# Gated mix of two attentions: the score maxima of two heads taken by one reduction over two adjacent PSUM banks

## The chip, the core and the metric

The kernel runs on one core of a Trainium2 chip. The metric is the device time of one launch in microseconds; lower is better. The core's engines work side by side, each through its own queue in order: TensorE (PE, with its weight loads listed apart as PEld), VectorE (DVE), ScalarE (ACT), GpSimd (POOL), and SyncE (SP), which issues most transfers. Matmuls write to PSUM, here used as eight banks of 128 partitions x 512 fp32 values.

## The reference

Two attentions are computed on the same input x (2048 tokens, width 512, 32 heads of 16), mixed by a gate per token:

```python
def _A_ref(x, wq, wk, wv, wo, beta):        # causal inside 4 segments of 512 tokens, plus a memory
    ...
    for s in range(N):
        logits = einsum("bhqd,bhkd->bhqk", qs, ks) * scale + mask
        p = softmax(logits); a_dot = einsum("bhqk,bhkd->bhqd", p, vs)
        num = einsum("bhld,bhde->bhle", phi(qs), M); den = einsum("bhld,bhd->bhl", phi(qs), z) + 1e-6
        outs.append(g * num / den + (1 - g) * a_dot)
        M = M + einsum("bhld,bhle->bhde", phi(ks), vs); z = z + phi(ks).sum()
    ...
def _B_ref(x, wqkv, wo):                    # full attention over 2048 tokens
    p = softmax(einsum("bhqd,bhkd->bhqk", q, k) * Dh ** -0.5)
    ...
g = sigmoid((x * gate_w).sum(-1, keepdims=True))
return g * _A_ref(...) + (1 - g) * _B_ref(...)
```

The softmax needs the maximum of each query's scores. The kernel computes the scores twice: once with the queries on the partitions, only for their maxima, and once transposed, with the maxima already subtracted inside the product, for the exponentials.

## The kernel before, in words

**Stages.** Up to about 366 us the projections, the memory part of attention A and the first maxima are computed. Then a long loop over k = 0..31 follows; step k of it (called a *unit* here) handles one set of four heads and 512 queries of attention B (number 32+k in the code) and one of attention A (number k). Units 0 to 30 have 25 *phases* each (`NPH`, p = 0..24). Unit 31 has no maxima left to compute and runs in another form, and a tail writes the last outputs.

**A phase** is one call of `step` and one of `pv_cols`. `step` emits two kinds of products. *T products* (`qk_mm`, L509; `a_unit`, L549 for attention A) are transposed scores of one head, 128 keys x 512 queries; ACT takes the exponential of each bank (L513, L552) and writes it to SBUF. There are three in a phase and they rotate over three banks, tb0, tb1 and mb. *S products* (`s_half`, L528; `s_a_half`, L425 for attention A) are scores of the *next* unit, 128 queries x 512 keys of one head, for the maxima; DVE reduces each bank to one maximum per query (L532; L445 and L447 for attention A). They rotate over four banks, sbk0 to sbk3 (`SK`, by `rot("s", SK)`). For attention A the causal mask is added by four small matmuls (`s_a_end`, L439 and L441) before the reduction. After `step`, `pv_cols` emits the *PV products* (`pv`, L626): exponentials times values, four heads at a time in four column groups, summed over the whole unit in the bank pvb.

**Row groups.** S and T products contract over only 64 partitions. `r = slice(64 * j, 64 * j + 64)` for an S product of half j, and `r = slice(64 * (h % 2), ...)` for a T product of head h, say which half of TensorE's rows it uses. An S item comes twice in the list of items, once for each half j, which are two heads. `step` asks for the half that is not the row group of the T product that follows (`s_item(f, 1 - n % 2)`).

**What sets the order.** It is written out by hand: the Python emits instructions in the order in which each engine runs them. `CP` says how many S products each phase holds: three in every phase, four in the last. `SAP` says which phases hold one of attention A's six items (phases 16, 7, 20, 13, 24, 0). From unit 9 on, phase `OMP` = 8 is followed by one output projection (`out_mm`, twelve full-width matmuls, L691) into a bank taken from the S rotation. Phase 13 ends with `m_chain` (L471, one small reduction on DVE), which marks one point of every unit in the trace. Phase 17 ends with `m_rows` (L488, small matmuls), and phases 1 and 22 with `fin_copy` (L635: ACT copies pvb out), which the next PV products wait for.

Of the kernel before, what the change touches and what calls it, by code (L numbers as in the profile page):

```python
# [7 lines left out]
FT = mybir.dt.float32  # L8
# [4 lines left out]
OP = mybir.AluOpType  # L13
AX = mybir.AxisListType
# [7 lines left out]
C = 512  # L22
# [10 lines left out]
def gated_mix_kernel(ctx, tc, x, wq, wk, wv, wo, beta, wqkv, wob, gate_w, out):  # L33
    nc = tc.nc
# [5 lines left out]
    PS = ctx.enter_context(tc.tile_pool(name="ps", bufs=1, space=PSUM))  # L40
# [41 lines left out]
    ones = P.tile([128, 1], FT, name="ones")  # L82
    MST = [[X.tile([128, 8, 32], FT, name=f"mst{i}{s}") for s in range(2)] for i in range(2)]

    TB = [PS.tile([128, C], FT, name=f"tb{i}") for i in range(2)]
    PVB = PS.tile([128, C], FT, name="pvb")
    MB = PS.tile([128, C], FT, name="mb")
    SK = [PS.tile([128, C], FT, name=f"sbk{i}") for i in range(4)]
    APVB = [PVB, MB]
    lru = []  # L90

# [4 lines left out]

    mode = {"misc": TB + [MB, PVB] + SK[::2]}

# [14 lines left out]
    def rot(key, lst):  # L113
        i = cnt.get(key, 0)
        cnt[key] = i + 1
        return lst[i % len(lst)]
# [301 lines left out]
    SAB = {}  # L418

    def s_a_half(u, i, p, j):  # L420
        n = 128 * (i + 1)
        b = SAB.setdefault((u, i, p), {})[j] = rot("s", SK)
        r = slice(64 * j, 64 * j + 64)
        for c0, q in [(0, p)] if p is not None else [(0, 0), (256, 1)]:
            nc.tensor.matmul(b[:, c0:c0 + n], q_of(u)[r, q, i * 128:(i + 1) * 128], k_of(u, q)[r, :n],  # L425
                             start=c0 == 0, stop=False, skip_group_check=True)

    def s_a_end(u, i, p):
        mx = pair_max(chain_of(u))
        n = 128 * (i + 1)  # L430
        bs = SAB.pop((u, i, p))
        np = 1 if p is not None else 2
        for n2 in (1, 0):
            for j in (1, 0):
                r = slice(64 * j, 64 * j + 64)
                d = bs[j].rearrange("q (p k) -> q p k", p=np)[:, :, n - 128 + 64 * n2:n]
                mv = cmask[r, n2, None, 64 * n2:].to_broadcast([64, np, 128 - 64 * n2])
                if n2:
                    nc.tensor.matmul(d, crows[r, 1], mv, start=False, stop=False, skip_group_check=True)  # L439
                else:  # L440
                    nc.tensor.matmul(d[:66], crows[r, 0, :66], mv, start=False, stop=True, skip_group_check=True)  # L441
        m = mx[:, 0].rearrange("q (j p) i -> q j p i", j=2)
        for j in bs:
            if np == 1:
                nc.vector.tensor_reduce(m[:, j, p, i:i + 1], bs[j][:, :n], axis=AX.X, op=OP.max)  # L445
            else:
                nc.vector.tensor_reduce(m[:, j, :, i], bs[j].rearrange("q (p k) -> q p k", p=2)[:, :, :n], axis=AX.X,  # L447
                                        op=OP.max)

    def s_a(u, i, p):  # L450
        for j in (1, 0):
# [3 lines left out]
    MXB = {}  # L455
# [63 lines left out]
    def s_half(t, j=None):  # L519
        u, i, p, kc = t  # L520
        js = HALF.setdefault(t, [1, 0])
        if j in js:
            js.remove(j)
        else:
            j = js.pop(0)
        b = rot("s", SK)
        r = slice(64 * j, 64 * j + 64)
        nc.tensor.matmul(b, q_of(u)[r, p, i * 128:(i + 1) * 128], k_of(u, p)[r, kc * C:(kc + 1) * C],  # L528
                         start=True, stop=True)
        if u not in MXB:  # L530
            MXB[u] = W.tile([128, 2, 2, 4, 4], FT, name="mxb")
        nc.vector.tensor_reduce(MXB[u][:, j, p, i, kc:kc + 1], b, axis=AX.X, op=OP.max)  # L532

    def s_item(f, j=None):
        if callable(f):
            f()
        elif f[0] == "A":
            s_a_half(*f[1:], j)
        else:
            s_half(f, j)  # L540
# [15 lines left out]

    NPH = 25

    def step(k, ns, items, banks):
        for n in ns:  # L560
            ends = None
            if items:
                f = items.pop(0)
                s_item(f, 1 - n % 2)
                if not callable(f) and f[0] == "A":
                    SEEN[f] = SEEN.get(f, 0) + 1
                    ends = f if SEEN[f] == 2 else None
            if n < 64:
                it, h = divmod(n, 4)
                b = bank(banks)  # L570
                qk_mm(32 + k, it, h, b)
                exp_b(32 + k, it, h, b)
            else:
                a_unit(k, n - 64, banks)
            if ends:
                s_a_end(*ends[1:])
        while items:
            f = items.pop(0)
            s_item(f)

    SEEN = {}

# [104 lines left out]
    def out_mm(c, t, a, b=None):  # L687

        b = misc() if b is None else b
        for n, (oi, wi, g) in enumerate([(oi, wi, g) for oi, wi in TERMS for g in range(4)]):  # L690
            nc.tensor.matmul(b, (AT["oh"], AT["ol"])[oi][:, g, a], (AT["wh"], AT["wl"])[wi][:, g, a],  # L691
                             start=n == 0, stop=n == 11)
        if a == 0:
            AT["yo"] = AT["L"].tile([128, DM], FT, name="yo")
            (nc.vector.tensor_copy if c == 2 and t == 3 else nc.scalar.copy)(AT["yo"], b)
        else:
            tt = 4 * c + t
            if tt == 11:
                nc.vector.tensor_tensor(AT["yo"], b, AT["yo"], op=OP.add)
            else:  # L700
                y2 = AT["L"].tile([128, DM], FT, name="y2")
                nc.scalar.activation(y2, b, AF.Copy)
                nc.gpsimd.tensor_tensor(AT["yo"], y2, AT["yo"], op=OP.add)
            nc.sync.dma_start(outr[tt * 128:(tt + 1) * 128, :], AT["yo"])
# [149 lines left out]
    for blk in range(16):  # L854
        g, c = divmod(blk, 4)
        pg, pc = divmod(blk - 1, 4)
        if blk == 4:
            mode["misc"] = TB + [MB, PVB]
        if 4 <= blk < 14:
# [5 lines left out]
        n = blk + 1 + (c == 2)  # L865
# [36 lines left out]
        for n in range(4):  # L902
# [9 lines left out]
            if nf == 35:  # L912
                mode["misc"] = [MB, PVB, TB[1]]
            if n < 3 and nf < want:
# [45 lines left out]

    T3 = TB + [MB]
    TAIL = [SK[n] for n in (2, 3, 0, 1)]
# [69 lines left out]

    ex = [extras(k) for k in range(32)]
    plan = {}
    CP = [3, 3, 3, 3, 3, 3, 3, 3, 3, 3, 3, 3, 3, 3, 3, 3, 3, 3, 3, 3, 3, 3, 3, 3, 4]
    PLAST = 14
    OM1, OM2 = 4, 10
    TMB = 18
# [14 lines left out]
    for k in range(31):  # L1053
# [15 lines left out]
        for n, t in enumerate(ST_A):  # L1069
            if True:  # L1070
                p = SAP[n]
# [35 lines left out]
    for k in range(32):  # L1107
        ua, ub = k, 32 + k
        if k == 31:
            for it in range(NT + 5):  # L1110
                step(k, range(4 * it, min(4 * it + 4, 74)), [], (T3 if it < NT - 4 else TB) + SK * (it < TMB) + TAIL[1:] * (it >= TMB))
                if it in (OM1, OM2):
                    out_mm(2, 3, int(it == OM2))
                n = it - 2
                if it == 0:
                    pv_cols(30, END - 256, END)
                    fin_copy(30)
                elif n >= 0:
                    lo, hi = (min(C * m, NT * C + (0, C, C + 512, C + 768)[max(m - NT, 0)]) for m in (n, n + 1))
                    pv_cols(k, lo, hi)  # L1120
                for a in TM.get(it, ()):
                    tail_mm(0, range(3), a)
                if n == NT - 1:
                    tail_hop(63)
                if it == 3:
                    m_chain(32)
                if it == 5:
                    m_rows(32)
                hooks(k, it)
            tail_hop(31)  # L1130
            continue
        done = 0
        for p in range(NPH):
            step(k, range(3 * p, min(74, 3 * p + 3)), list(plan.get((k, "p", p), [])), T3)
            if p < 2:
                if k:
                    pv_cols(k - 1, END - (512 if p == 0 else 256), END - (256 if p == 0 else 0))
                if k and p:
                    fin_copy(ua - 1)
            else:  # L1140
                to = 384 * (p - 1) if p < 22 else NT * C + 384 * (p - 22)
                if k == 30 and p == NPH - 1:
                    to = END - 256
                pv_cols(k, done, to)
                done = to
                if p == 22:
                    fin_copy(ub)
            if p == OMP and k > 8:
                fin_rec(31 + k)
                fin_rec(k - 1)  # L1150
                out_mm((k - 9) // 8, (k - 9) // 2 % 4, (k - 9) % 2, rot("s", SK))
            if p == MRP:
                m_rows(k + 1)
            if p == PLAST - 1:
                m_chain(k + 1)
            for it in range(3 * p // 4, 3 * (p + 1) // 4) if p < 24 else (18,):
                hooks(k, it)
    for h in range(2):
        for a in (1, 0):
            cs = slice(256 * h, 256 * h + 256)  # L1160
            d, o = AT["d"][a][64:, cs], AT["o"][1][64:, 3, a, cs]
# [41 lines left out]
```

## Time and profile before

| | |
|---|---|
| time, median of 2 runs | 1849.84 us (1848.86 to 1850.81) |
| the profiled execution | 1852.35 us, of which its span is 1850.6 us |
| granted TensorE clock | 0.999 |
| PE busy | 1838.5 us (99%), 17541 matmuls |
| DVE busy | 1603.9 us (87%), 2868 instructions |
| ACT busy | 1403.1 us (76%), 2734 instructions |
| DVE, maxima of attention B (L532) | 2048 reductions of 128x512, 1246.4 us |
| DVE, maxima of attention A (L445, L447) | 384 reductions, 211.7 us |

A busy PE is not a PE at its peak: the ends of matmuls are modelled, and a matmul that waits inside a row group counts as busy. So PE is read by the distance from one group of instructions to the next, not by its busy share. Times in the timeline are in us from the start of the span; a row merges equal instructions that follow each other closely, x giving how many.

### The profile page before, as it was taken

The numbers are of one execution on the slowest core, as the hardware profiler recorded it, in microseconds if no ns is written. First come the engines' busy times: TensorE is split into PE (matmuls) and PEld (weight loads), VectorE is DVE, ScalarE is ACT, GpSimd is POOL, SyncE is SP. The second block draws the span as 40 slices with busy tenths as digits, with TensorE's granted clock in tenths as the row PEclk, the third lists the DMA queues.
The fourth block names the chain that finished last, engine by engine and source line by source line (L and its number), as shares of the span: only waits on it lengthen the run. The fifth ranks groups of instructions, "written<-read, shape, count | busy, mean of one in ns | idle before, by whom it ended". The sixth has DMA issues, their size and how long they took to land. (4 is left out here: it accounts for less than half of the span.)

```text
span 1850.6 us, 45423 instructions
## 1 busy us (share of the span) xinstructions
PE 1838.5 (99%) x17541; PEld 1003.1 (54%) x17541; DVE 1603.9 (87%) x2868; ACT 1403.1 (76%) x2734; POOL 342.8 (19%) x722
## 2 busy tenths in 40 slices
PE   9999999999999999999999999999999999999999
PEld 7887777544444444555555555555555555555545
DVE  6145776999999999999999999999999999999953
ACT  4233333688888888888888888888888888888894
POOL 3100001112221111121212121121212121212122
PEclk9999999999999999999999999999999999999999
DMA  6576665543534343434343434343434343424211
GB/s 227 156 206 199 192 197 185 156 110 98 128 98 118 90 122 89 111 96 113 95 114 97 116 98 116 97 116 92 122 92 122 91 123 87 124 82 122 69 48 44
DMA packets 181735, 220.00 MB, mean 119 GB/s; under 512 B 42360, under 2 KB 93064, under 8 KB 181328
## 3 DMA queue, kind: packets, MB, share of 16 engines
q1 hardware_dynamic: 178336, 208.32, 40.6%
q0 software_dynamic: 2480, 8.13, 1.4%
q8 instruction: 139, 2.28, 0.5%
q10 hardware_dynamic: 704, 0.66, 0.1%
q14 instruction: 76, 0.62, 0.1%
HBM read 148.07 MB, written 67.64 MB: 117 GB/s over the span
## 5 line engine op out<-in xcount | busy, mean ns | idle before, releaser
L532 DVE TENSOR_REDUCE mxb<-sbk 128x1 f32<-128x512 f32 x2048 | 1246.4, 680 | 49.0 <-PE tb L509 41.8
L513 ACT ACTIVATE raw<-tb 128x512 f32<-128x512 f32 x904 | 505.9, 599 | 88.3 <-PE tb L509 64.1
L528 PE MATMUL sbk<-xh,qb 64*128 64x512 f32 x1344 | 461.8, 442 | 0.5
L626 PE MATMUL pvb<-raw,vb 128*17 128x384 f32 (+3 forms) x5216 | 401.1, 394 | 0.0
L528 PEld LDWEIGHTS sbk<-xh,qb 64*128 64x128 f32 x1344 | 219.5, 185 | 238.6 <-DVE mxb L532 149.2
L509 PE MATMUL tb<-qb,xh 64*128 64x512 f32 x878 | 332.0, 450 | 0.0
L513 ACT ACTIVATE pb<-tb 128x512 f32<-128x512 f32 x447 | 252.8, 599 | 44.8 <-PE tb L509 31.1
L513 ACT ACTIVATE raw<-mb 128x512 f32<-128x512 f32 x437 | 265.4, 607 | 0.3 <-PE tb L509 0.3
L528 PE MATMUL sbk<-kb,qb 64*128 64x512 f32 x704 | 233.0, 441 | 0.0
L626 PE MATMUL pvb<-pb,vb 128*17 128x128 f32 (+3 forms) x2600 | 208.7, 393 | 0.0
L509 PE MATMUL mb<-qb,xh 64*128 64x512 f32 x426 | 190.5, 447 | 0.0
L509 PE MATMUL tb<-qb,kb 64*128 64x512 f32 x473 | 180.1, 452 | 0.0
L626 PEld LDWEIGHTS pvb<-raw,vb 128*17 128x17 f32 x5216 | 106.0, 96 | 136.5 <-issue 107.6
L528 PEld LDWEIGHTS sbk<-kb,qb 64*128 64x128 f32 x704 | 109.9, 184 | 119.3 <-DVE mxb L532 69.7
L445 DVE TENSOR_REDUCE mx<-sbk 128x1 f32<-128x512 f32 (+1 forms) x256 | 146.5, 614 | 6.6 <-PE sbk L441 4.1
L509 PEld LDWEIGHTS tb<-qb,xh 64*128 64x128 f32 x878 | 137.6, 184 | 4.0 <-ACT raw L513 1.6
L425 PE MATMUL sbk<-ka,qa 64*128 64x256 f32 (+3 forms) x512 | 133.8, 353 | 0.0
L513 ACT ACTIVATE pb<-mb 128x512 f32<-128x512 f32 x220 | 133.5, 607 | 0.3 <-PE mb L509 0.3
L554 POOL TENSOR_SCALAR_AFFINE_SELECT raw<-raw 128x256 f32<-128x256 f32 (+1 forms) x212 | 76.7, 362 | 240.3 <-ACT raw L552 234.8
L425 PEld LDWEIGHTS sbk<-ka,qa 64*128 64x128 f32 x512 | 70.3, 185 | 86.5 <-DVE mxb L532 70.0
L509 PE MATMUL mb<-qb,kb 64*128 64x512 f32 x231 | 103.9, 450 | 0.5 <-DVE st L290 0.5
L653 POOL TENSOR_TENSOR rec<-rec,grow 128x16 f32<-128x16 f32 x62 | 13.9, 224 | 472.5 <-DVE rec L650 435.6
(303 smaller groups left out, 2476.3 us busy)
## 6 DMA issues: line engine op xcount, KB each, us to landing
xh<-dB SPq DMA_DIRECT2D x168, 128.0 KB
vb<-vdB SPq DMA_DIRECT2D x16, 1088.0 KB
dB<-st SPq DMA_DIRECT2D x64, 256.0 KB
dA<-st SPq DMA_DIRECT2D x64, 256.0 KB
pd<-pvs SPq DMA_DIRECT2D x62, 256.0 KB
xh<-dB SPq DMA_DIRECT2D x168, 64.0 KB
kb<-dB SPq DMA_DIRECT2D x80, 128.0 KB
qb<-dB SPq DMA_DIRECT2D x64, 128.0 KB
```

What stands on the lines that cost most here:

```text
L425: nc.tensor.matmul(b[:, c0:c0 + n], q_of(u)[r, q, i * 128:(i + 1) * 128], k_of(u, q)[r, :n], start=c0 == 0, stop=False, skip_group_check=True)
L445: nc.vector.tensor_reduce(m[:, j, p, i:i + 1], bs[j][:, :n], axis=AX.X, op=OP.max)
L509: nc.tensor.matmul(b, k_of(u, h // 2)[r, 128 * it:128 * it + 128], q_of(u)[r, h // 2], start=True, stop=True)
L513: nc.scalar.activation(pt, b, AF.Exp, scale=SCALE)
L528: nc.tensor.matmul(b, q_of(u)[r, p, i * 128:(i + 1) * 128], k_of(u, p)[r, kc * C:(kc + 1) * C], start=True, stop=True)
L532: nc.vector.tensor_reduce(MXB[u][:, j, p, i, kc:kc + 1], b, axis=AX.X, op=OP.max)
L554: nc.gpsimd.affine_select(out=m, in_=m, pattern=[[1, 128]] if n < 4 else [[0, 2], [1, 128]], compare_op=OP.is_ge, fill=0.0, base=0, channe ...
L626: nc.tensor.matmul(APVB[u == 31][32 * h:32 * h + E + 1, q0 + lo:q0 + hi], vt[:, it, 4 * q + h, :], pt[:, lo:hi], start=it == 0 and lo == 0 ...
L653: nc.gpsimd.tensor_tensor(r, r, grow[:, int(kd == "B"), c], op=OP.mult)
```

## The change

All eight PSUM banks become one tile, `G` (128 x 8 x 512). Banks 4 to 7 keep their uses (tb0, tb1, mb, pvb), and banks 0 to 3 are cut into two *pairs*, `SP`. The two halves j of an S item are written into the two banks of one pair, and when both are there one reduction reads the pair and writes two maxima per query. The S rotation thus has two places of two banks where it had four of one. The output projection of phase 8 takes the first bank of a pair.

Phases now hold four and two S products in turn (`CP`). A table `PATS` gives the order of S and T products in a phase: S S T T T S S where there are four, T S T S T where there are two. As before an S product asks for the half opposite to the next T product in the list, and where that half has been used it takes the other. For attention A the masks are added after the T product that follows the second half.

```diff
-    TB = [PS.tile([128, C], FT, name=f"tb{i}") for i in range(2)]
-    PVB = PS.tile([128, C], FT, name="pvb")
-    MB = PS.tile([128, C], FT, name="mb")
-    SK = [PS.tile([128, C], FT, name=f"sbk{i}") for i in range(4)]
+    G = PS.tile([128, 8, C], FT, name="sbk")
+    TB = [G[:, 4], G[:, 5]]
+    MB, PVB = G[:, 6], G[:, 7]
+    SP = [G[:, 0:2], G[:, 2:4]]
+    SK = [b[:, j] for b in SP for j in range(2)]
...
     def s_a_half(u, i, p, j):
         n = 128 * (i + 1)
-        b = SAB.setdefault((u, i, p), {})[j] = rot("s", SK)
+        if (u, i, p) not in SAB:
+            SAB[u, i, p] = rot("s", SP)
+        b = SAB[u, i, p][:, j]
...
         m = mx[:, 0].rearrange("q (j p) i -> q j p i", j=2)
-        for j in bs:
-            if np == 1:
-                nc.vector.tensor_reduce(m[:, j, p, i:i + 1], bs[j][:, :n], axis=AX.X, op=OP.max)
...
+        nc.vector.tensor_reduce(m[:, :, slice(p, p + 1) if np == 1 else slice(0, 2), i], bs[:, :, :, :n], axis=AX.X, op=OP.max)
...
     def s_half(t, j=None):
...
-        b = rot("s", SK)
+        if t not in SAB:
+            SAB[t] = rot("s", SP)
+        b = SAB[t][:, j]
...
-        nc.vector.tensor_reduce(MXB[u][:, j, p, i, kc:kc + 1], b, axis=AX.X, op=OP.max)
+        if not js:
+            nc.vector.tensor_reduce(MXB[u][:, :, p, i, kc], SAB.pop(t), axis=AX.X, op=OP.max)
...
+    PATS = {4: "SSTTTSS", 2: "TSTST"}
+
     def step(k, ns, items, banks):
-        for n in ns:
-            ends = None
-            if items:
+        ns, items = list(ns), list(items)
+        o = PATS.get(len(items), "") if len(ns) == 3 else ""
+        o = o or "ST" * min(len(ns), len(items)) + "T" * (len(ns) - len(items)) + "S" * (len(items) - len(ns))
+        n, ends = (ns or [0])[0], None
+        for ch in o:
+            if ch == "S":
+                n = ns[0] if ns else n
                 f = items.pop(0)
                 s_item(f, 1 - n % 2)
...
-    CP = [3, 3, 3, 3, 3, 3, 3, 3, 3, 3, 3, 3, 3, 3, 3, 3, 3, 3, 3, 3, 3, 3, 3, 3, 4]
+    CP = [4, 2] * 12 + [4]
...
-                out_mm((k - 9) // 8, (k - 9) // 2 % 4, (k - 9) % 2, rot("s", SK))
+                out_mm((k - 9) // 8, (k - 9) // 2 % 4, (k - 9) % 2, rot("s", SP)[:, 0])
```

On TensorE, two plain phases of a unit before, up to the PV rows of the second (L528 are S products, L509 T products, L626 the PV products; the names left of the arrow are PSUM banks):

```order
L528 MATMUL sbk_121<-xh_88,qb_69 128x512
L509 MATMUL tb_115<-qb_70,kb_89 128x512
L528 MATMUL sbk_118<-xh_88,qb_69 128x512
L509 MATMUL mb<-qb_70,kb_89 128x512
L528 MATMUL sbk_119<-xh_88,qb_69 128x512
L509 MATMUL tb_114<-qb_70,kb_89 128x512
L626 MATMUL pvb<-raw_86,vb_2972 17x384 x4
L528 MATMUL sbk_120<-xh_88,qb_69 128x512
L509 MATMUL tb_115<-qb_70,kb_89 128x512
L528 MATMUL sbk_121<-xh_88,qb_69 128x512
L509 MATMUL mb<-qb_70,kb_89 128x512
L528 MATMUL sbk_118<-xh_88,qb_69 128x512
```

The same work now (L507 are T products, L636 the PV products; every bank is part of the tile sbk):

```order
L528 MATMUL sbk<-xh_87,qb_68 128x512 x2
L507 MATMUL sbk<-qb_70,kb_89 128x512 x3
L528 MATMUL sbk<-xh_87,qb_68 128x512 x2
L636 MATMUL sbk<-raw_86,vb_2916 17x384 x4
L507 MATMUL sbk<-qb_70,kb_89 128x512
L528 MATMUL sbk<-xh_87,qb_68 128x512
L507 MATMUL sbk<-qb_70,kb_89 128x512
L528 MATMUL sbk<-xh_87,qb_68 128x512
L507 MATMUL sbk<-qb_70,kb_89 128x512
L636 MATMUL sbk<-raw_86,vb_2916 17x128 x4
```

Two blocks of six products each have become one of seven and one of five; the PV products between them are the same. On DVE, around the two small reciprocals that follow phase 8, before:

```order
L532 TENSOR_REDUCE mxb_9531<-sbk0_118 128x1
L532 TENSOR_REDUCE mxb_9531<-sbk1_119 128x1
L532 TENSOR_REDUCE mxb_9531<-sbk2_120 128x1
L532 TENSOR_REDUCE mxb_9531<-sbk3_121 128x1
L650 RECIPROCAL rec_9753<-rec_9753 128x16
L650 RECIPROCAL rec_9848<-rec_9848 128x16
L532 TENSOR_REDUCE mxb_9531<-sbk1_119 128x1
```

and now:

```order
L446 TENSOR_REDUCE mx_8529<-sbk_114 128x2
L533 TENSOR_REDUCE mxb_8492<-sbk_114 128x2 x2
L660 RECIPROCAL rec_8702<-rec_8702 128x16
L660 RECIPROCAL rec_8792<-rec_8792 128x16
L533 TENSOR_REDUCE mxb_8492<-sbk_114 128x2 x6
```

One reduction with two results stands where two with one result stood; what is between them has not moved.

More of the change, by code (lines that the diff above doesn't have):

```diff
@@ L430, in s_a_end @@
         n = 128 * (i + 1)
-        bs = SAB.pop((u, i, p))
+        bs = SAB.pop((u, i, p)).rearrange("q j (p k) -> q j p k", p=2 - (p is not None))
         np = 1 if p is not None else 2
@@ L435, in s_a_end @@
                 r = slice(64 * j, 64 * j + 64)
-                d = bs[j].rearrange("q (p k) -> q p k", p=np)[:, :, n - 128 + 64 * n2:n]
+                d = bs[:, j, :, n - 128 + 64 * n2:n]
                 mv = cmask[r, n2, None, 64 * n2:].to_broadcast([64, np, 128 - 64 * n2])
@@ L442, in s_a_end @@
         m = mx[:, 0].rearrange("q (j p) i -> q j p i", j=2)
-        for j in bs:
-            if np == 1:
[L445 to L448, printed above, removed]
+        nc.vector.tensor_reduce(m[:, :, slice(p, p + 1) if np == 1 else slice(0, 2), i], bs[:, :, :, :n], axis=AX.X, op=OP.max)
     def s_a(u, i, p):
@@ L566, in step @@
                     SEEN[f] = SEEN.get(f, 0) + 1
-                    ends = f if SEEN[f] == 2 else None
+                    ends = f if SEEN[f] == 2 else ends
+                if ends and not ns:
+                    s_a_end(*ends[1:])
+                    ends = None
+                continue
+            n = ns.pop(0)
             if n < 64:
@@ L576, in step @@
                 s_a_end(*ends[1:])
-        while items:
-            f = items.pop(0)
-            s_item(f)
+                ends = None
     SEEN = {}
```

## The prediction

> **What bounds the kernel now.** I read the busy times first, then stretches between the marks that L471 leaves once a unit, then the timeline inside a phase.
>
> ```profile
> PE 1838.5 (99%) x17541; PEld 1003.1 (54%) x17541; DVE 1603.9 (87%) x2868; ACT 1403.1 (76%) x2734; POOL 342.8 (19%) x722
> ...
> 365.91 0.22 DVE L471 TENSOR_REDUCE mx<-mxb 128x16 f32<-128x64 f32 x1
> 725.52 0.22 DVE L471 TENSOR_REDUCE mx<-mxb 128x16 f32<-128x64 f32 x1
> 1764.09 0.22 DVE L471 TENSOR_REDUCE mx<-mxb 128x16 f32<-128x64 f32 x1
> ...
> 365.90:725.50 359.60, 359.51 (x3872) 169.36 (x3864) 359.08 (x632) 318.76 (x617) 64.81 (x158) 1.00 0.40 107
> 725.50:1764.10 1038.60, 1038.60 (x10911) 523.02 (x10909) 991.10 (x1739) 888.04 (x1717) 207.61 (x439) 1.00 0.39 103
> ```
>
> The last two rows give PE, PEld, DVE, ACT and POOL busy, the granted clock (1.00) and DMA. The eight *early* units, before the output projections begin, take 359.61/8 = 44.95 us each, and DVE is busy for 359.08 of 359.60: DVE is their bound. The 22 *late* units take 1038.57/22 = 47.21, and DVE is idle 47.5/22 = 2.16 in each. ACT is at 89% and 86%. So whatever shortens DVE's list helps early units until the next engine is reached. That engine is PE, whose own pace has to be read from phases:
>
> ```profile
> 1008.01 0.49 PE L528 MATMUL sbk<-xh,qb 64*128 64x512 f32 x1
> 1008.01 0.72 PE L509 MATMUL tb<-qb,xh 64*128 64x512 f32 x2
> 1008.35 0.61 PE L528 MATMUL sbk<-xh,qb 64*128 64x512 f32 x2
> 1008.58 0.38 PE L509 MATMUL mb<-qb,xh 64*128 64x512 f32 x1
> 1008.90 0.84 PE L626 MATMUL pvb<-pb,vb 128*17 128x384 f32 x8
> 1009.67 0.49 PE L528 MATMUL sbk<-xh,qb 64*128 64x512 f32 x1
> ...
> 1783.00 0.73 PE L509 MATMUL sbk<-qb,xh 64*128 64x512 f32 x4 [0.17 <-DVE mx L447]
> 1783.66 0.63 PE L626 MATMUL pvb<-raw,va 128*17 128x256 f32 x8
> ...
> 999.95 6.67 DVE L532 TENSOR_REDUCE mxb<-sbk 128x1 f32<-128x512 f32 x11 [2.12 <-PE tb L509]
> ```
>
> A block of three S and three T products takes 1008.01 to 1008.90 = 0.89, and its PV products 0.77 more: a phase of 1.66. Six products start at three moments (1008.01, .35, .58), two at a time, one in each row group. I call such a moment a *slot*. Four T products, two slots, take 0.66 (1783.00 to 1783.66), so a slot is worth 0.89 - 0.66 = 0.23. Eleven reductions take 6.67, the last one 0.68: one starts every (6.67 - 0.68)/10 = 0.599. Two phases hold six, 3.59 on DVE, against 3.32 on PE. PE has 0.27 to spare in two phases, no more.
>
> **The change, on DVE.** The trace has no reduction over two banks. These rows bound it:
>
> ```profile
> L445 DVE TENSOR_REDUCE mx<-sbk 128x1 f32<-128x512 f32 x116 | 74.2, 680 | 0.0
> L445 DVE TENSOR_REDUCE mx<-sbk 128x1 f32<-128x384 f32 x116 | 58.7, 547 | 0.0
> L447 DVE TENSOR_REDUCE mx<-sbk 128x2 f32<-128x512 f32 x58 | 37.4, 688 | 1.0
> ```
>
> 128 elements cost 133 ns, so 512 more cost 0.53, and a second result 8 ns: 0.69 + 0.53 = 1.22 long. Reductions in a row overlap by 0.680 - 0.599 = 0.08, so one pair starts every 1.14, where two singles take 1.20. The upper bound is two whole singles, 1.20 apart (nothing won), or 1.28 if crossing banks also costs the overlap. The lower one is the elements alone, 1.07. I take 1.14, from the nearest row (two results, one bank). A unit has 32 pairs of attention B and six of A: 38 x 0.06 = 2.2 saved, and DVE's list falls from 44.95 to about 42.8.
>
> The Trainium skill, in "VectorE: DVE Perf Modes", section "The TRN2 errata", puts a VectorE instruction that reads PSUM at 120 cycles plus one per element, 0.66 us for 512 and 1.19 for 1024. The trace agrees on a single one (0.68). By the page alone a pair would save 0.125, 4.8 a unit. The trace has the reductions overlap, which leaves 0.06 to save, and the trace decides.
>
> **On PE.** The instructions are the same, their order is not. By the rows in the code and the order above, the block of seven runs S1 S0 T0 T1 T0 S1 S0 (the number is the row group). Row group 0 has four products, row group 1 three, so it needs four slots. The block of five runs T1 S1 T0 S0 T1: the S product stands behind a T product of its own row group, so T1 is alone, then S1 with T0, then S0 with T1: three slots. Two phases that took six slots take seven: 0.23 more in 3.32, which makes 3.55. That a product alone costs a whole slot is shown here, where ACT has delayed a third T product:
>
> ```profile
> 1772.10 0.50 PE L509 MATMUL mb<-qb,kb 64*128 64x512 f32 x1
> 1772.49 0.49 PE L509 MATMUL tb<-qb,kb 64*128 64x512 f32 x1
> 1772.91 0.84 PE L626 MATMUL pvb<-raw,vb 128*17 128x128 f32 x16
> ```
>
> It stands alone and PV begins 0.42 after it, where after a last pair PV begins 0.32 later (1008.58 to 1008.90). The 0.10 between is its weight load, which came late; none of it is shared.
>
> So a plain double phase goes from 3.59 (DVE) to 3.55 (PE): the gain on DVE is eaten by PE. For whole units I need PE's own list, which is the unit less the time in which DVE holds PE. Twelve double phases give 12 x 0.27 = 3.3, less what the phases of a unit hold beside plain ones:
>
> ```profile
> 1006.24 0.44 PE L425 MATMUL sbk<-ka,qa 64*128 64x384 f32 x1
> 1007.24 0.84 PE L626 MATMUL pvb<-raw,vb 128*17 128x384 f32 x8
> ...
> 1770.01 0.39 PE L488 MATMUL tb<-ident,m 128*32 128x128 f32 x4
> 1770.33 0.44 PE L425 MATMUL sbk<-ka,qa 64*128 64x384 f32 x1
> ...
> 1031.14 0.50 PE L528 MATMUL sbk<-xh,qb 64*128 64x512 f32 x1
> 1032.38 0.13 PEld L626 LDWEIGHTS pvb<-raw,vb 128*17 128x17 f32 x8 [0.31 <-ACT pvs L635]
> ...
> 1026.42 0.80 PE L528 MATMUL sbk<-xh,qb 64*128 64x512 f32 x2
> 1027.14 0.30 PE L626 MATMUL pvb<-raw,va 128*17 128x128 f32 x4
> ```
>
> Masks lengthen a block to 1.00, 0.11 more, six times: 0.66. `m_rows` takes 0.32. The phase that waits for ACT to copy pvb has a block of 1.24, 0.35 more. That leaves 3.3 - 1.33 = 2.0. In phase 24 a pair of S products stands 0.72 before PV instead of 0.32: 0.40 more in which DVE holds PE. PE's own list is thus 44.95 - 2.4 = 42.55. The change adds 12 x 0.23 = 2.76, of which the wait for the copy hides one slot (0.23; without that wait it would count too): 45.1. An early unit is PE's then, 45.1 against 44.95.
>
> In late units the output projection comes on top:
>
> ```profile
> 1043.66 1.20 PE L691 MATMUL sbk<-wh,oh 128*128 128x512 f32 x4
> 1046.60 0.50 PE L528 MATMUL sbk<-xh,qb 64*128 64x512 f32 x1
> 1047.13 1.89 DVE L532 TENSOR_REDUCE mxb<-sbk 128x1 f32<-128x512 f32 x3 [2.07 <-PE tb L509]
> ```
>
> It takes PE 2.94, while DVE lives on its backlog and then idles 2.07. Before, 0.9 of it was thus free. With PE the bound all 2.94 count: 45.1 + 2.94 = 48.0, against 47.2. It takes a pair, so the phase behind it has the other pair only; ACT frees the bank in some 0.7 after the last matmul (1046.60 to 1046.71 + 0.59), a phase before it is needed.
>
> **The wait that is added.** With two places, the S products of one pair wait for the reduction of the pair before the last, and T and PV products queue behind them. The tightest is the second pair of the block of seven, which needs the reduction of the pair in the block of five. That pair's last product starts 0.57 into its block and its scores are ready at about 1.0 (1046.60 to 1047.13 is 0.53 for a first slot). With 1.22 for the reduction the banks are free at 2.2. The waiting product is due at 1.66 + 0.57 = 2.23, and has until 2.46, since its partner has to wait for the fourth slot anyway. So it costs nothing while a pair takes less than about 1.4. ACT has six exponentials to do in 3.55, one every 0.48 (two take 1.08, one 0.60):
>
> ```profile
> 1008.57 1.08 ACT L513 ACTIVATE raw<-tb 128x512 f32<-128x512 f32 x2 [0.22 <-PE tb L509]
> ```
>
> that is 2.9, and three banks carry the T T T. The tile that holds all banks adds no wait if dependences follow the addresses; DMAs and POOL keep their order. The first 366 us and the end are PE's, whose list is unchanged there: nothing.
>
> **Sum.** About 8.7 early units (the first one counts in part) x 0.15 = 1.3, and 22 x 0.8 = 17.6: 19 us more. The profiled execution, 1852.35 (span 1850.6), would be 1871; the median 1849.84 becomes 1869.
>
> **Rivals.** *Faster: a product alone costs nothing.* If TensorE fills the odd slot (with PV's weight loads, say), DVE's 42.8 and PE's 42.55 stand: early units 2.1 less, late ones 45.5 at best, 1.7 less: -18 - 37 gives 1795. The row of 0.42 speaks against it, and for it only that PV's loads were not ready then.
>
> *Slower: a product alone costs more than a slot.* Where a product follows one of its own row group with nothing beside it, its weight load may lie bare, 0.10 as at 1772.49. Twelve times in 30.7 units is 37 us: 1906. It passes 2% from 0.05 each. Against it stands this row, a load for a row group that is computing:
>
> ```profile
> 1008.12 0.41 PEld L528 LDWEIGHTS sbk<-xh,qb 64*128 64x128 f32 x2
> ```
>
> It runs from 1008.12, under products of 1008.01 that fill both row groups, and the next slot starts on time. The Trainium skill, in "TensorE: Matmul & The Clock Gate", section "The mechanism", says that a weight load overlaps running matmuls only where the row group differs. By that every slot would carry a bare load, before as after, and this row disagrees.
>
> *Slower: two banks cost as two reductions.* At 1.20 DVE's list is 44.95 again, PE's 45.1, and each delays the other: some 0.5 a unit, 1885. At 1.28 DVE gains 38 x 0.08 = 3.0 a unit, about 1940.
>
> *It doesn't do what it says*: waits on the one tile could be coarser than banks. The rows of the order show the merged reductions, and this would cost far more than 2%.
>
> **How the numbers follow.** A difference of 2%, 37 us, is about what a measurement here can surely tell from no change. The forecast, 1869, has 0.66, nearly all of it within 2% (0.62; 0.04 above). The product that costs nothing has 0.13, all faster. The bare load has 0.12, slower in 0.10 of it. Two banks as two have 0.07, half of it slower, and coarse waits 0.02. Together 0.13 faster, 0.68 the same, 0.19 slower. The range leaves out the faster rival and the dearest cases: from 1840, where half of DVE's gain (1.05 in 8.7 early units, 9 us) gets through and late units lose nothing, to 1906.
>
> **What would show it.** Right: L471 marks 45.1 apart early and 48.0 late; DVE idle in early units too, some 2 us each; reductions of 128x1024 at 1.22 us; a block of seven at 1.12 and one of five at 0.89, with PV 0.77. Wrong: blocks of five at 0.80 or less (the odd slot shared), blocks over 1.25 with weight loads between products, or S products held by DVE in each block of seven.

## The result: 3.4% slower

The changed kernel takes 1912.85 us (median; 1912.18 to 1913.51), the kernel before 1849.84. The ratio is 1.0345, with an interval of 1.0329 to 1.0362. The forecast was 1869, its range 1840 to 1906: the sign of the sum was right, its size was not.

The page of the changed kernel, its busy times and the row of the merged reductions:

```profile
PE 1889.8 (99%) x17541; PEld 1024.9 (54%) x17541; DVE 1569.8 (82%) x1652; ACT 1405.1 (74%) x2734; POOL 344.0 (18%) x722
...
L533 DVE TENSOR_REDUCE mxb<-sbk 128x2 f32<-128x1024 f32 x1024 | 1205.7, 1220 | 94.8 <-PE sbk L528 72.7
```

1024 merged reductions of 1.22 us stand where 2048 of 0.68 stood. DVE's busy time falls from 1603.9 to 1569.8, and the time gets longer all the same. The marks of units 0, 8 and 30 (the line was L471 before, it is L469 now):

```profile
360.92 0.22 DVE L469 TENSOR_REDUCE mx<-mxb 128x16 f32<-128x64 f32 x1
...
733.04 0.21 DVE L469 TENSOR_REDUCE mx<-mxb 128x16 f32<-128x64 f32 x1
...
1823.25 0.21 DVE L469 TENSOR_REDUCE mx<-mxb 128x16 f32<-128x64 f32 x1
```

An early unit takes (733.04 - 360.92)/8 = 46.52 (before 44.95), a late one (1823.25 - 733.04)/22 = 49.56 (before 47.21). The forecast said 45.1 and 48.0. The engines between these marks (PE, PEld, DVE, ACT, POOL busy, then the granted clock):

```profile
360.90:733.00 372.10, 369.20 (x3874) 177.57 (x3872) 350.09 (x328) 319.51 (x616) 65.10 (x158) 1.00 0.39 103
733.00:1823.30 1090.30, 1082.23 (x10914) 536.00 (x10914) 969.66 (x904) 889.82 (x1717) 208.39 (x439) 1.00 0.38 99
```

DVE idles 22.0/8 = 2.75 in an early unit, where before it hardly idled at all. PE is the bound now, at a clock of 1.00, but for some waits at the unit's edge that are shown below. Inside a plain double phase (the timeline, columns as before):

```profile
1058.71 0.49 PE L528 MATMUL sbk<-xh,qb 64*128 64x512 f32 x2
1059.05 0.39 PE L507 MATMUL sbk<-qb,kb 64*128 64x512 f32 x2
1059.28 0.39 PE L528 MATMUL sbk<-xh,qb 64*128 64x512 f32 x1
1059.28 0.39 PE L507 MATMUL sbk<-qb,kb 64*128 64x512 f32 x1
1059.52 0.39 PE L528 MATMUL sbk<-xh,qb 64*128 64x512 f32 x1
1059.83 0.63 PE L636 MATMUL sbk<-raw,vb 128*17 128x256 f32 x8
...
1060.61 0.51 PE L507 MATMUL sbk<-qb,kb 64*128 64x512 f32 x2
1060.94 0.40 PE L528 MATMUL sbk<-xh,qb 64*128 64x512 f32 x2
1061.18 0.42 PE L507 MATMUL sbk<-qb,kb 64*128 64x512 f32 x1
1061.53 0.84 PE L636 MATMUL sbk<-pb,vb 128*17 128x384 f32 x8
1062.30 0.50 PE L528 MATMUL sbk<-xh,qb 64*128 64x512 f32 x2
```

The block of seven lasts 1058.71 to 1059.83, 1.12, in four slots, and its last product stands alone. The block of five lasts 0.92, in three. With its PV products the double phase takes 1062.30 - 1058.71 = 3.59, where 3.55 was forecast. So the plain parts are as forecast, and a unit is 1.4 to 1.6 longer than was made of them. At the unit's edge, where four halves follow on four (phases 24 and 0), PE waits:

```profile
1049.93 1.23 DVE L446 TENSOR_REDUCE mx<-sbk 128x4 f32<-128x1024 f32 x1 [0.58 <-PE sbk L444]
1051.07 1.22 DVE L533 TENSOR_REDUCE mxb<-sbk 128x2 f32<-128x1024 f32 x1
1051.21 0.32 PE L428 MATMUL sbk<-ka,qa 64*128 64x128 f32 x1 [0.31 <-DVE mx L446]
...
1052.34 0.19 PEld L528 LDWEIGHTS sbk<-xh,qb 64*128 64x128 f32 x2 [0.37 <-DVE mxb L533]
```

Phase 0 waits 0.31 for the merged maximum of attention A, and the weight load of its second pair waits 0.37 for one of attention B.

The first mark also moves, from 365.91 to 360.92: the beginning is 5.0 us shorter, where the forecast had put nothing.

### The profile page after: what moved, and what is told of

Read it like the earlier page. It is cut to its first block, busy times and chain, and to the rows that moved or that the text cites. A ratio compares the mean times of both kernels' runs of the same rounds, so it can differ in the third digit from the quotient of the medians.

```text
span 1910.5 us, 44180 instructions
## 1 busy us (share of the span) xinstructions
PE 1889.8 (99%) x17541; PEld 1024.9 (54%) x17541; DVE 1569.8 (82%) x1652; ACT 1405.1 (74%) x2734; POOL 344.0 (18%) x722
## 4 chain that ended last, share of the span: by engine, by line
PE 89%; DVE 4%; DMA 3%; ACT 2%; SPq 1%; issue 1%; POOL 0%; ACTq 0%; DVEq 0%
PE sbk L636 29%; PE sbk L507 17%; PE sbk L528 16%; PE sbk L280 9%; PE sbk L265 5%; PE sbk L701 4%; PE sbk L428 3%; PE sbk L550 2%; DVE mxb L533 2%; DVE mx L446 2%; PE sbk L749 1%; PE sbk L444 1%; DMA xh<-dB 1%; PE sbk L442 1%; ACT raw L511 1%
## 5 line engine op out<-in xcount | busy, mean ns | idle before, releaser
L533 DVE TENSOR_REDUCE mxb<-sbk 128x2 f32<-128x1024 f32 x1024 | 1205.7, 1220 | 94.8 <-PE sbk L528 72.7
L511 ACT ACTIVATE raw<-sbk 128x512 f32<-128x512 f32 x1368 | 731.9, 602 | 129.2 <-PE sbk L507 72.8
L511 ACT ACTIVATE pb<-sbk 128x512 f32<-128x512 f32 x680 | 370.3, 603 | 61.8 <-PE sbk L507 33.9
L636 PE MATMUL sbk<-raw,vb 128*17 128x384 f32 (+3 forms) x5216 | 400.4, 394 | 0.0
L507 PE MATMUL sbk<-qb,xh 64*128 64x512 f32 x1344 | 381.5, 448 | 0.0
L528 PE MATMUL sbk<-xh,qb 64*128 64x512 f32 x1344 | 345.7, 436 | 2.0 <-DVE mxb L533 0.8
L507 PEld LDWEIGHTS sbk<-qb,xh 64*128 64x128 f32 x1344 | 183.1, 184 | 156.5 <-ACT raw L511 81.3
L446 DVE TENSOR_REDUCE mx<-sbk 128x2 f32<-128x1024 f32 (+2 forms) x192 | 200.6, 1046 | 64.3 <-PE sbk L444 28.2
L636 PE MATMUL sbk<-pb,vb 128*17 128x128 f32 (+3 forms) x2600 | 208.7, 393 | 0.0
L528 PEld LDWEIGHTS sbk<-xh,qb 64*128 64x128 f32 x1344 | 151.9, 184 | 104.8 <-issue 76.2
L507 PE MATMUL sbk<-qb,kb 64*128 64x512 f32 x704 | 201.8, 448 | 0.8 <-DVE st L291 0.8
L636 PEld LDWEIGHTS sbk<-raw,vb 128*17 128x17 f32 x5216 | 106.0, 96 | 150.6 <-issue 120.3
L528 PE MATMUL sbk<-kb,qb 64*128 64x512 f32 x704 | 177.1, 436 | 0.6
L507 PEld LDWEIGHTS sbk<-qb,kb 64*128 64x128 f32 x704 | 96.7, 184 | 81.7 <-ACT raw L511 60.8
L553 ACT ACTIVATE raw<-sbk 128x512 f32<-128x512 f32 x212 | 113.9, 608 | 8.8 <-PE sbk L550 6.3
L528 PEld LDWEIGHTS sbk<-kb,qb 64*128 64x128 f32 x704 | 77.5, 184 | 55.1 <-issue 39.7
```

The costliest lines, as they stand in the source:

```text
L446: nc.vector.tensor_reduce(m[:, :, slice(p, p + 1) if np == 1 else slice(0, 2), i], bs[:, :, :, :n], axis=AX.X, op=OP.max)
L507: nc.tensor.matmul(b, k_of(u, h // 2)[r, 128 * it:128 * it + 128], q_of(u)[r, h // 2], start=True, stop=True)
L511: nc.scalar.activation(pt, b, AF.Exp, scale=SCALE)
L533: nc.vector.tensor_reduce(MXB[u][:, :, p, i, kc], SAB.pop(t), axis=AX.X, op=OP.max)
L553: nc.scalar.activation(pt, b, AF.Exp, scale=SCALE)
L636: nc.tensor.matmul(APVB[u == 31][32 * h:32 * h + E + 1, q0 + lo:q0 + hi], vt[:, it, 4 * q + h, :], pt[:, lo:hi], start=it == 0 and lo == 0 ...
```

## The experiments

Two theories were to be told apart. *F*: the forecast's slack was right, and what failed is that waits for pairs were taken as free. *P*: the slack was too large; PE's own list in a unit, without any wait for DVE, was longer already before. A third, that the merging itself costs the time, was tested beside them.

**DVE's load taken away from the kernel before.**

```diff
-        nc.vector.tensor_reduce(MXB[u][:, j, p, i, kc:kc + 1], b, axis=AX.X, op=OP.max)
+        nc.vector.tensor_reduce(MXB[u][:, j, p, i, kc:kc + 1], b[:, :256], axis=AX.X, op=OP.max)
```

> The kernel before, with each maximum of attention B read over 256 of its 512 columns; the other half of the keys is left out of B's maxima, all products stay. DVE's list falls far below PE's, so the run shows PE's own list in a unit, which the forecast put at 42.55 early and 45.5 late. Theory F (the forecast's slack was right, and what failed is that the pairs' waits were taken as free): 8.7 x 2.4 + 22 x 1.7 = 58 less, about 1792. Theory P (the slack was too large; PE's list before is the changed kernel's measured 46.5 and 49.5 less the 2.53 of the twelve odd products, 44.0 and 47.0): 8.7 x 0.95 + 22 x 0.2 = 13 less, about 1837. A value between the two splits the miss between them.

Measured: 1830.24, 0.9893 of before (0.9876 to 0.9909). The windows between its marks:

```profile
359.80:711.10 351.30, 351.30 (x3880) 176.21 (x3878) 238.85 (x633) 318.87 (x617) 64.89 (x158) 1.00 0.42 109
711.10:1741.50 1030.40, 1030.40 (x10915) 527.33 (x10911) 656.76 (x1739) 886.24 (x1716) 207.79 (x439) 1.00 0.40 104
```

DVE is busy for two thirds of the time and PE for all of it: units of 351.3/8 = 43.91 and 1030.4/22 = 46.84 are PE's own list, with its waits for ACT in it. The forecast had 42.55 and 45.5. It is 1.36 and 1.34 too low, which is most of the miss. Theory P holds, and the slack of the kernel before was 1.04 early and 0.37 late, not 2.4 and 1.7.

**DVE's load taken away from the changed kernel.**

```diff
-            nc.vector.tensor_reduce(MXB[u][:, :, p, i, kc], SAB.pop(t), axis=AX.X, op=OP.max)
+            nc.vector.tensor_reduce(MXB[u][:, :, p, i, kc], SAB.pop(t)[:, :, :256], axis=AX.X, op=OP.max)
```

> The changed kernel, with each merged maximum of attention B read over 256 columns of both banks; half of the keys is left out of B's maxima, all products and their order stay. The merged reduction falls from 1.22 to about 0.69, so PE should hardly wait for it. Theory F (waits for the pairs are the miss): the forecast's 45.1 and 48.0 appear, about 1868. Theory P (PE's own list is the miss): nothing is won, 1905 to 1913.

Measured: 1904.85, 1.0297 (1.0281 to 1.0312). Its windows:

```profile
360.50:730.70 370.20, 367.73 (x3878) 177.19 (x3876) 226.45 (x328) 319.99 (x618) 64.91 (x158) 1.00 0.40 104
730.70:1814.10 1083.40, 1076.58 (x10914) 534.11 (x10913) 625.28 (x903) 889.64 (x1717) 207.79 (x439) 1.00 0.38 99
```

Units of 46.28 and 49.25: waits for maxima of attention B are worth 0.24 early and 0.31 late, 8 us in all. Against before_half the new order costs 46.28 - 43.91 = 2.37 early and 49.25 - 46.84 = 2.41 late, where the forecast had 2.53. A wait for a maximum of attention A, which this edit leaves whole, is still in it:

```profile
1045.74 1.23 DVE L446 TENSOR_REDUCE mx<-sbk 128x4 f32<-128x1024 f32 x1 [1.12 <-PE sbk L444]
1047.02 0.33 PE L428 MATMUL sbk<-ka,qa 64*128 64x128 f32 x1 [0.31 <-DVE mx L446]
```

The mean length of blocks (first S or T product to the first PV product; in phase 18 from `m_rows` on, 0.32 before) over the late units shows where both go:

| block of phase | before | before_half | after_half | after |
|---|---|---|---|---|
| 0 | 1.15 | 1.28 | 1.24 | 1.56 |
| 2 | 1.25 | 1.29 | 1.27 | 1.43 |
| 3 | 1.13 | 1.13 | 0.97 | 0.96 |
| 4 | 0.90 | 0.89 | 1.12 | 1.13 |
| 6 | 0.90 | 0.90 | 1.13 | 1.13 |
| 10 | 0.99 | 0.99 | 1.23 | 1.23 |
| 14 | 0.89 | 0.89 | 1.11 | 1.11 |
| 18 | 1.22 | 1.30 | 1.44 | 1.44 |
| 24 | 1.37 | 1.08 | 1.08 | 1.08 |
| PV of 24, with the wait behind it | 0.81 | 0.80 | 1.16 | 1.16 |
| all 25 phases | 47.20 | 46.85 | 49.20 | 49.51 |

From before_half to after_half each block of seven away from the edge is 0.14 to 0.25 longer (the ten together 2.13), and blocks 0 and 2 are not (something else was late there already). The edge adds 0.36 for the maximum of A, then 0.31 more for those of B (blocks 0 and 2 longer, block 1 shorter).

**The order alone.**

```diff
+    PATS = {4: "SSTTTSS", 2: "TSTST"}
...
-    CP = [3, 3, 3, 3, 3, 3, 3, 3, 3, 3, 3, 3, 3, 3, 3, 3, 3, 3, 3, 3, 3, 3, 3, 3, 4]
+    CP = [4, 2] * 12 + [4]
```

> The kernel before with its single reductions and its four separate banks, but with the products in the changed kernel's order, steps of four and two halves in turn. Here the two halves of a masked tile always go to different row groups. Theory F (odd products cost 2.53 a unit, the pairs' waits the rest): about 1868. Theory P (the order alone is the whole loss): 1905 to 1913. Third theory (the merged reductions make the loss, the order is free): about 1850.

Measured: 1921.06, 1.0383 (1.0368 to 1.0399). The order alone is more than the whole loss. Its units are 46.77 and 49.71 long. Since its masked halves go to different row groups, its partner among the merged kernels is after_fix below, 1915.15: merging the maxima is a small gain in this order, not the loss. In the mean over late units blocks 1 to 24 agree with those of after_fix within 0.015, so neither the one tile nor the pairs add a wait there. The difference is at the edge, where blocks of phase 0 take 2.05 (1.56 in after_fix), while the stretch from PV of phase 24 on takes 0.80 (1.16 there). In phase 0 PE waits for a single reduction:

```profile
1057.34 1.28 DVE L532 TENSOR_REDUCE mxb<-sbk 128x1 f32<-128x512 f32 x2
...
1058.67 0.18 PEld L528 LDWEIGHTS sbk<-xh,qb 64*128 64x128 f32 x1 [0.38 <-DVE mxb L532]
```

**The masked tiles' halves.**

```diff
-            s_a_half(*f[1:], j)
+            s_a_half(*f[1:], 1 - SEEN.get(f, 0))
```

> The changed kernel, with one thing mended: in its phases 0, 16 and 20 both halves of a masked tile get the same n and so the same row group, which computes one head's half twice and leaves the other head's out of the maxima. Here the second half goes to the other head. By the slot count nothing changes: S1 S1 T0 T1 T0 S1 S0 and S1 S0 T0 T1 T0 S1 S0 both need four slots, so 1913 within 5. If two products of one row group in a row cost a slot more than two of different ones, three slots of 0.23 a unit come back: 30.7 x 0.69 = 21 less, 1892.

Measured: 1915.15, 1.0355 (1.0340 to 1.0371); the changed kernel's interval overlaps it. What was said of the change, that a product takes the other half where the wanted one has been used, holds for attention B alone: in phases 0, 16 and 20 the changed kernel leaves out one half of a masked tile's maxima and computes the other twice. This moves some 2 us: block 20 goes from 1.17 to 1.23 with the halves put right, and no other block by more than 0.01. So the changed kernel's time may be read as that of the order. The rival's 1892 is refuted: two products of one row group in a row are no dearer as such, as long as the longer list of the two groups stays the same.

**An eighth product in the empty place.**

```diff
         if not js:
+            if TWICE[0]:
+                r, b = slice(64 * (1 - j), 64 * (1 - j) + 64), SAB[t][:, 1 - j]
+                nc.tensor.matmul(b, q_of(u)[r, p, i * 128:(i + 1) * 128], k_of(u, p)[r, kc * C:(kc + 1) * C],
+                                 start=True, stop=True)
...
+                TWICE[0] = o == PATS[4] and not items
                 s_item(f, 1 - n % 2)
+                TWICE[0] = False
```

> The changed kernel with its masked tiles mended as in after_fix, and in every block of seven one product more: the last pair's first half is computed again, with the same operands into the same bank, behind the last half, in the row group that stands empty there. 367 products of 512 columns more, twelve in a unit. Slot theory (an odd product pays for a slot of 0.23 whose other row group is empty): the added products stand in the empty places and cost nothing, within 6 of after_fix's 1915. Rival (each product has a price of its own, half a slot, whether paired or not): 367 x 0.115 = 42 more, 1957.

Measured: 1930.48, 1.0440 (1.0424 to 1.0456): 15 us above after_fix, between the two. A plain block (L537 is the added product):

```profile
1040.87 0.50 PE L530 MATMUL sbk<-xh,qb 64*128 64x512 f32 x2
1041.20 0.63 PE L507 MATMUL sbk<-qb,xh 64*128 64x512 f32 x3
1041.44 0.39 PE L530 MATMUL sbk<-xh,qb 64*128 64x512 f32 x1
1041.67 0.39 PE L537 MATMUL sbk<-xh,qb 64*128 64x512 f32 x1
1041.67 0.39 PE L530 MATMUL sbk<-xh,qb 64*128 64x512 f32 x1
1042.00 0.52 PE L644 MATMUL sbk<-pb,vb 128*17 128x384 f32 x4
```

It runs beside the last product and the block still takes 1.13: the place was empty and is free to fill. In the means over late units, against after_fix, that holds for nine of the twelve blocks of seven. Block 0 is longer by 0.23, block 8 by 0.15 and block 18 by 0.09, no other by more than 0.03: 0.47 a unit, 14 of the 15 us. Why these three pay was not tested; in block 0 the pair whose first half is computed again is one that already waits for its banks.

**An odd product made in every block of the kernel before.**

```diff
-                s_item(f, 1 - n % 2)
+                s_item(f, n % 2)
```

> The kernel before, with each half of a maxima pair put into the row group of the T product behind it and not into the other one. The instructions and their number are the same; a block of three S and three T takes four slots and not three (S0, T0 with S1, T1 with S0, T0). Slot theory, on PE's own lists as before_half measured them (43.9 early, 46.85 late): 24 x 0.23 = 5.5 a unit more, 49.4 and 52.35, so 8.7 x 4.45 + 22 x 5.15 = 152 more, about 2001. Rival (an odd product costs half a slot): 2.75 a unit, 46.7 and 49.6, about 1917.

Measured: 1977.92, 1.0696 (1.0674 to 1.0717): 129 us more, 152 expected for a whole slot, 68 for half a slot. A plain block:

```profile
1063.88 0.51 PE L528 MATMUL sbk<-xh,qb 64*128 64x512 f32 x2
1064.21 0.41 PE L509 MATMUL tb<-qb,xh 64*128 64x512 f32 x2
1064.44 0.39 PE L528 MATMUL sbk<-xh,qb 64*128 64x512 f32 x1
1064.67 0.39 PE L509 MATMUL mb<-qb,xh 64*128 64x512 f32 x1
1065.00 0.52 PE L626 MATMUL pvb<-pb,vb 128*17 128x384 f32 x4
```

Four starts, the first two 0.33 apart and the others 0.23, and 1.12 in place of 0.89: a slot is 0.22 to 0.23. Units are 48.57 and 51.56, 4.7 above before_half, not 5.5. Blocks 2 and 3, which wait for ACT there already, are no longer than in before_half (1.26 and 1.13) and hide a whole slot each; blocks that took 0.95 to 0.99 for another reason (phases 5, 10, 12, 15) take the same 1.12 and hide a part; block 0 takes 0.42 more.

**The four-on-four moved from the unit's edge to the output projection.**

```diff
-    CP = [4, 2] * 12 + [4]
+    CP = [4, 2] * 4 + [4, 4] + [4, 2] * 7 + [2]
```

> The changed kernel, but the steps that stand four after four are moved from the unit's edge (phases 24 and 0) to phases 8 and 9, where the output projection of a late unit stands between them; phase 24 gets two. Theory (pairs make PE wait only where eight halves come in two phases on end: blocks 0 and 2 are 0.32 and 0.16 shorter in after_half than in the changed kernel): late units lose 0.3 to 0.5, early ones little, since there nothing stands between phases 8 and 9: 22 x 0.3 to 0.5 is 7 to 11 less, 1902 to 1906. Rival (the waits are spread over the unit, or move along): 1913 or more.

Measured: 1905.85, 1.0306 (1.0290 to 1.0321), 7 us below the changed kernel. The list in the edit puts four halves into phases 8, 9 and 10, so that 10 follows on 9 with no output projection between them, which the expectation left out. Its windows:

```profile
362.90:736.20 373.30, 371.77 (x3882) 179.76 (x3884) 349.66 (x329) 320.58 (x619) 64.77 (x158) 1.00 0.41 104
736.20:1817.10 1080.90, 1080.07 (x10914) 540.24 (x10912) 967.45 (x904) 891.89 (x1717) 207.63 (x439) 1.00 0.39 99
```

A late unit falls by 49.56 - 49.13 = 0.43. Block 0 goes back to 1.24 and the PV products of phase 24 to 0.79, while block 9, a block of seven now, and block 10 take 0.30 and 0.21 more. An early unit, which has no projection, rises by 0.14. The edge waits are real and can be moved, but they are the smaller part of the loss.

**Pairs without the order of four and two.** In merge_within a tile is merged where both its halves stand in one phase; merge_only merges all:

```diff
+        SPLIT.update(f for f in items if items.count(f) == 1)
...
+        if t not in SPLIT:
+            if not js:
+                nc.vector.tensor_reduce(MXB[u][:, :, p, i, kc], SAB.pop(t), axis=AX.X, op=OP.max)
+        else:
+            nc.vector.tensor_reduce(MXB[u][:, j, p, i, kc:kc + 1], b, axis=AX.X, op=OP.max)
...
```

> Pairs without the order of four and two: the changed kernel's banks in one tile and its merged maxima, but with the order of the kernel before (three halves a phase, S T S T S T). Where both halves of a tile stand in one phase they are merged (two tiles of three, and the masked ones); where they stand in two phases each half keeps its own reduction. Theory A (merging is harmless, the order alone is the loss): DVE's list falls by 27 x 0.06 = 1.6, PE's own 43.9 and 46.85 show, 8.7 x 1.04 + 22 x 0.37 = 17 less than before, 1832. Theory B (in this order a pair gives its banks back too late: the reduction starts at its second half, 0.35 behind the first, and holds both banks for 1.22): slower than before, between 1850 and 1980, with PE waiting for maxima.

> One part of the change alone: the tile of eight banks and all merged maxima, with the order of the kernel before (three halves a phase). Every third pair then stands in two phases, with PV products of 0.77 between its halves. Theory (a pair that straddles PV holds one bank for a whole phase without work for DVE, and PE runs into it): slower than merge_within's 1975, 2000 to 2200. Rival (only merging is new, DVE's shorter list shows): below 1850.

Measured: merge_within 1974.78, 1.0685 (1.0667 to 1.0703); merge_only 2147.79, 1.1606 (1.1583 to 1.1629). In merge_within a block of phase 14:

```profile
1055.30 0.68 DVE L538 TENSOR_REDUCE mxb<-sbk 128x1 f32<-128x512 f32 x1
1055.37 0.49 PE L530 MATMUL sbk<-xh,qb 64*128 64x512 f32 x1
...
1056.03 0.18 PEld L530 LDWEIGHTS sbk<-xh,qb 64*128 64x128 f32 x1 [0.48 <-DVE mxb L538]
1056.70 0.52 PE L633 MATMUL sbk<-pb,vb 128*17 128x384 f32 x4
```

The block's second half waits for a bank and all behind it queue: 1.33 in place of 0.89. In merge_only the waits for maxima are the first row of the waits of PE's weight loads (microseconds in all, times, longest):

```profile
PEld sbk L528 <- DVE mxb L533: 485.5, 650, 1.9
```

So merging needs both halves in one phase and their pair of banks free by then; the order of four and two gives that, and costs the odd slots.

**Where PE's own list was longer than thought.** Half of the keys is left out as in before_half, and the copies of the PV accumulator go to DVE:

```diff
-        if u == 30:
+        if u != 31:
             nc.vector.tensor_copy(ps, PVB)
```

> before_half (half of the keys left out of B's maxima), with the two copies of the PV accumulator in a unit moved from ACT, where they stand among the exponentials, to DVE, which is idle there. It asks where PE's own list is longer than the forecast made it: in before_half blocks 2 and 3, behind the first copy, take 1.29 and 1.13 where a plain one takes 0.89. Theory (ACT falls behind by its copies and gives T banks back late, in block 3 too, which the forecast left out): blocks 2 and 3 lose 0.3 to 0.6 together, 30.7 x 0.3 to 0.6 is 9 to 18 less than before_half's 1830, 1812 to 1821. Rival (those blocks are long for another reason, or DVE gives the copy no sooner): 1830 or more.

Measured: 1825.41, 0.9873 (0.9853 to 0.9892); 5 us below before_half, less than expected. The two intervals overlap, so the times alone would not tell the two kernels apart; between the marks a unit is 0.20 shorter, early and late. Blocks 2 and 3 in before_half:

```profile
1015.03 0.62 ACT L635 ACTIVATE pvs<-pvb 128x512 f32<-128x512 f32 x1
...
1015.21 0.18 PEld L509 LDWEIGHTS mb<-qb,kb 64*128 64x128 f32 x1 [0.20 <-ACT raw L513]
...
1015.70 0.13 PEld L626 LDWEIGHTS pvb<-raw,vb 128*17 128x17 f32 x8 [0.30 <-ACT pvs L635]
...
1017.17 0.18 PEld L509 LDWEIGHTS mb<-qb,kb 64*128 64x128 f32 x1 [0.17 <-ACT pb L513]
```

and in half_copy:

```profile
1011.64 0.69 DVE L633 COPY pvs<-pvb 128x512 f32<-128x512 f32 x1
...
1012.31 0.18 PEld L509 LDWEIGHTS mb<-qb,kb 64*128 64x128 f32 x1 [0.20 <-ACT raw L513]
...
1012.73 0.13 PEld L626 LDWEIGHTS pvb<-raw,vb 128*17 128x17 f32 x8 [0.24 <-DVE mxb L532]
...
1013.50 0.72 PE L509 MATMUL tb<-qb,kb 64*128 64x512 f32 x2
...
1014.08 0.39 PE L509 MATMUL mb<-qb,kb 64*128 64x512 f32 x1
1014.40 0.13 PEld L626 LDWEIGHTS pvb<-raw,vb 128*17 128x17 f32 x8 [0.37 <-issue]
```

Block 3 falls from 1.13 to 0.89: its third T product had waited 0.17 for a bank that ACT gave back late, one phase after the copy. Blocks 4 and 6 take 0.06 more each; why was not tested. Block 2 loses only 0.05. In half_copy its copy ends at 1012.33, and PV still begins only at 1012.73, 0.42 after the third T product, as after the late one at 1772.49 in the kernel before. So it is this product that makes block 2 long: in both kernels it starts 0.80 into the block, where a plain one starts at 0.57, and its weight load waits 0.20 for ACT's exponentials (the rows of 1015.21 and 1012.31). The copy adds only some 0.06.

No kernel here that does all the work is faster than the one before.

## Why the prediction was wrong, point by point

**DVE: right.** A pair is 1.22 long, as worked out from two results in one bank, and DVE stopped being the bound.

**The slot: right in its size, a little too many of them.** A block of seven takes 1.12, one of five 0.92; fill_seven shows the odd place empty and lone_before prices a slot at 0.22 to 0.23. The sum had 2.53 a unit; the runs show 2.41 in a late unit, of which 0.36 is a wait, so some 2.05: a slot is hidden in block 2 (as said) and in block 0 too. The Trainium skill, in "TensorE: Matmul & The Clock Gate", section "The mechanism", says that a weight load overlaps running matmuls only where the row group differs. The added product of fill_seven disagrees again: its load ran from 1041.44 on, under products of both row groups, and it started at 1041.67, a slot of 0.23 after them.

**PE's own list: the step that failed.** It was "the unit less the time in which DVE holds PE", 44.95 - 2.4 = 42.55. The 2.4 came from one plain double phase, twelve times 0.27, less masks, `m_rows` and one wait for ACT's copy, plus 0.40 for phase 24. before_half measured 43.91, so the slack was 1.04. A small part of the miss lies in where the slack was counted from: 0.27 takes a start every 0.599 on DVE for all 76 reductions, 45.5 a unit, while a whole unit lasts 44.95, since some of attention A's maxima are shorter (0.55 over 384 columns). The forecast's own rows for PE, added up, give 25 x 1.66 + 1.33 = 42.83, 0.28 more than 42.55. The other 1.08 is in the phases that are not plain, which were undercounted. In late units of before_half, against plain blocks of 0.89 and what the forecast allowed for beside them: block 0 has 0.28 more (1.28, against 0.89 and 0.11 of masks), block 3 has 0.24 (which half_copy takes away), blocks 10 and 18 have 0.10 and 0.09, the PV products of phase 22 have 0.21 (0.98 against 0.77), and blocks 5, 12, 15 and 23 have 0.06 each. Together that is 1.16. Over all 25 phases the blocks hold 1.31 more than was allowed, and the stretches from PV on 0.23 less (PV takes 0.56 in phases 0 and 1). Only for block 3 is the cause shown: the copy keeps ACT from giving a bank back in time. Phase 24 in turn gave back 0.29, not 0.40. The 0.35 allowed for block 2 was right in its size, but it was put down to the wait for the copy, which adds 0.06; the rest is the third T product, which waits for its bank.

**The added wait: wrong at one place.** "It costs nothing" holds in the middle of the unit, where the pair in the block of seven comes in time. It was worked out for a seven behind a five. At the edge four halves follow on four, and there stands a maximum of A with four results, 1.23 long: 0.36 and 0.31 in a late unit.

**The output projection: right.** 2.94 was said; before_half has 46.84 - 43.91 = 2.93, the changed kernel 3.04.

A late unit thus goes from the 48.0 forecast to 49.56 by 1.34 (PE's list) - 0.48 (slots) + 0.36 + 0.31 (waits) = 1.53. Over 8.7 early and 22 late units PE's list is 1.36 x 8.7 + 1.34 x 22 = 41 us, about the whole difference of 44 between 1869 and 1913 (41 between 1871 and 1912.18, the profiled executions). The waits and the hidden slots largely cancel; what they leave, some 5 us, is about what the beginning gives back. There the forecast put nothing, on the ground that PE is the bound, and the first mark comes 5.0 us earlier. In before_half, with DVE relieved, it also comes earlier, at 359.8, so DVE had held PE there too.

**The rivals.** The slower rival of 0.10 for a bare load came to 1906, closer to the time than the forecast, by a mechanism that isn't there: blocks of seven take 1.12, not 1.22. Two banks do not cost as two reductions (the second of two pairs starts 1.13 behind the first, where two singles take 1.20), and the one tile made no coarse waits (order_only, with separate banks, has the same blocks away from the edge). "A product alone costs nothing" is refuted by lone_before.

## What to carry to other kernels

The slack of an engine behind the bound is not read from the smoothest phase times the number of phases. Add up the engine's own list phase by phase, the irregular ones above all, or make the bounding engine's work cheaper in one run and look at what is left: with before_half's 43.91 and 46.84 for PE's list, the forecast's own 2.53 would have given 8.7 x 1.49 + 22 x 2.16 = 60 more, 1910. Row-tiled products are counted by row group in each stretch between two full-height ones, and an odd one costs the whole slot. A merged reader gives its buffers back together, so the place to check is the densest one, not the mean.

## What the runs showed of the hardware that was not expected

A product does not wait for the one that stands before it in the program for the other row group. The block of five is T S T S T in the program, and the forecast put its first T alone; in the trace the two first T products start together (1060.61, two in 0.51), then the two S products (1060.94), then the last T. lone_before shows the same: S T S T S T in the program, and S S, T T, S, T in the trace. In these blocks each row group works off its own list, and the longer one sets the length. What was said of the chip at the start, that each engine's queue runs in order, thus holds for these products of TensorE only within a row group. The Trainium skill, in "TensorE: Matmul & The Clock Gate", section "The mechanism", says that matmuls start strictly in program order; these rows disagree with it.

A reduction of two results over two banks is no dearer than one of as many elements would be: 1.22 for 1024, against 0.69 for two results of 256 in after_half and 0.68 for one of 512. Back to back the pairs still overlap:

```profile
1060.39 2.35 DVE L533 TENSOR_REDUCE mxb<-sbk 128x2 f32<-128x1024 f32 x2
```

Two take 2.35, so the second starts 1.13 behind the first. As two singles take 1.20, merging is worth 0.06 to 0.07 of DVE, which is all that there was to win, and a slot of 0.22 to 0.23 on PE was paid for every three pairs, which are what two phases hold.
